# Recurrence: v asked for ahead of the decays, k and r; w1's loads one pair later; combining's first steps behind the diagonals in the last pair

## The chip, the cores and the metric

The kernel runs on one core of one Trainium2 chip. The metric is the device time of one execution in microseconds (us). Three executions of the kernel before took 430.78, 430.81 and 433.74 us (median 430.81).

## What is computed

Three layers, one after the other: a linear recurrence over 768 steps for 4 batches and 8 heads of 48 channels, a soft mixture of 8 experts with 4 slots each, and a dense block with a gated activation.

```python
for t in range(S):                       # S = 768, head_dim 48, float32
    cur = einsum('bhd,bhe->bhde', u * kt, vt)
    y[:, :, t] = einsum('bhd,bhde->bhe', rt, state + cur)
    state = wt * state + einsum('bhd,bhe->bhde', kt, vt)
logits = x @ phi                         # x: 3072 tokens x 384
d = softmax over tokens(logits)          # dispatch: 32 slots
slot_out[e] = relu(slot_input[e] @ w1[e]) @ w2[e]
c = softmax over slots(logits)           # combine
h = (c @ slot_out) @ w_in
out = (h * sigmoid(1.702 * h)) @ w_out
```

## The kernel before

**Stages.** `phase_a` is the recurrence with the logits of the mixture beside it, `phase_b` the experts, `phase_c` the dense block. The change lies in `phase_a` alone. The order of instructions on every engine is the order in which the code is written; nothing reorders it.

**A pair.** The recurrence is cut into 16 pairs: one batch, two heads, all 768 tokens in six chunks of 128. The loop over `i` (L650) interleaves pair `i` with the steps that prepare pair `i+1` and finish pair `i-1`. For one `i` the steps are, with the engine that does each:

- `products(i+1)` (L498 to L501, DVE): two scans over the decays z.
- `diagonal(i, 0)` and `diagonal(i, 3)` (L534, ACT): six activations each that write diagonal matrices `am`; `causal` (L568, DVE) lays the masked `scores` (L562, PE) over them.
- `states(i)` (L549, PE, then a scan L552 on DVE): 10 matmuls that read `v` of pair i. They stand on PE's queue in front of `outputs(i-1, 3)`.
- `outputs(i-1, 0)` and `outputs(i-1, 3)` (L579 reads `am` and `v` of pair i-1, L584 the states and `r`), with a copy L587 on ACT.
- `scale(i+1)` (L507, DVE), `coef(i+1)` (L520, PE), `coef_tr(i+1)` (L527, DVE), and on POOL `unscaled` (L492), the product of r and k in two halves. The small copies `beside` (L487) hold a POOL product back until a named DVE instruction has ended.
- `x_tr(i-1)` (L600, PE; L601, ACT) and `logits` (L810, PE).

**Loads.** All of them are issued by SP, in the order of the code, and an issue that waits holds up those behind it. `load_z` (L466, decays of pair i+3, two buffers), `load_rk` (L473, k and r of pair i+3, four buffers), `load_v` (L480, v of pair i+1, two buffers). So `load_v(i+1)` overwrites v of pair i-1 and has to wait for `outputs(i-1, 3)`; `load_rk(i+3)` overwrites k and r of pair i-1 and waits for the L584 of the same step. Pair 15's k and r are loaded late, at i = 13, for lack of a buffer. The weights w1 (L79, 512 KB each, three in two pairs), w_in (L114, pairs 8 to 13), and at the end w2 (L92) and w1's last expert (L85) fill the gaps.

**The last pair.** At i = 15 `combining` (L886) of the first two batches starts: maximum, difference (DVE L890, L891) and exponential (ACT L892) for each; its second part comes behind `causal(15, 3)`.

The functions that the change touches:

Of the kernel before, what the change touches and what calls it, by code (L numbers as in the profile page):

```python
# [44 lines left out]
NW1 = 7  # L45
# [231 lines left out]
def keep_warm(nc, room, idle, n):  # L277

    for _ in range(n):
        nc.tensor.matmul(room, idle[:, 512:640], idle[:, 0:512], start=True, stop=True)  # L280
# [138 lines left out]
def phase_a(tc, rkz, z0, vin, u_sb, prod, ebias, W, after, late, consts, soft):  # L419
# [5 lines left out]
    with ExitStack() as ctx:  # L425
# [31 lines left out]
        def load_z(p):  # L457
            if p >= n_p:
                return
            st.setdefault(p, {})["z"] = zs[p % 2]  # L460
            if p == 0:
                for c in halves_of_z[::-1]:
                    nc.sync.dma_start(out=zs[0][:, c], in_=z0[:, c])
                return
            for j in range(2):
                nc.sync.dma_start(out=zs[p % 2][64 * j:64 * j + D, :], in_=rkz[p, j, :, 2 * S:])  # L466
# [9 lines left out]
        def load_v(p):  # L476
            if p >= n_p:
                return
            v = vp.tile([128, VW], F32, name="v", bufs=2)
            nc.sync.dma_start(out=v, in_=vin[p])  # L480
            st[p]["v"] = v
# [47 lines left out]
        def diagonal(p, c0):  # L529
            q = st[p]  # L530
            am = q["am", c0] = ap.tile([128, 2, 3, CH], F32, name="am", bufs=3)
            for c in range(3):
                for j in range(2):
                    nc.scalar.activation(am[:, j, c], ident, AF.Copy, scale=q["coef"][:, c0 + c, j:j + 1])  # L534
# [115 lines left out]
        for i in range(n_p + 1):  # L650
            cur, nxt, prv = i < n_p, i + 1 < n_p, 1 <= i
            b1, b2 = batch_of(i - 2), batch_of(i - 3)
            if b2:
                next(peak)
                b2.exponentials()
            elif 2 <= i:
                logits(i - 2)
            if cur and i:
                diagonal(i, 0)
            if cur:  # L660
                keys_tr(i)
            if nxt:
                products(i + 1)
                load_z(i + 3)
            if cur:
                scores(i, 0)
            if b2 and i < n_p - 2:
                b2.token_major()
            if nxt:
                decays(i + 1)  # L670
            peak = b1.peak() if b1 else iter(())
            if prv:
                outputs(i - 1, 0)
            if b1:
                b1.read()
            if b2:
                logits(i - 2)
            if nxt:
                beside(x[:, XL - 1:XL])
                unscaled(i + 1, 1)  # L680
            if cur:
                causal(i, 0)
                states(i)
            next(peak, None)
            if i == n_p - 1:
                rooms = iter([room[:, n * 3 * CH:(n + 1) * 3 * CH] for n in range(3)])
                comb = [bat[1].combining(lambda: sp.tile([128, 3 * CH], F32, name="c4", bufs=3)),
                        bat[0].combining(lambda: next(rooms))]
                for it in comb:
                    next(it)  # L690
            if i == 0:
                keep_warm(nc, psT.tile(), idle, WARM1)
            if cur and i:
                diagonal(i, 3)
            if prv:
                outputs(i - 1, 3)
            if cur:
                scores(i, 3)
            if nxt:
                scale(i + 1)  # L700
            if i < n_p - 4:
                load_rk(i + 3)
            elif i == n_p - 3:
                load_rk(n_p - 1)
            if nxt:
                coef(i + 1)
            if i + 2 < n_p:
                beside(st[i + 1]["rk"][:, S - 1:S])
                unscaled(i + 2, 0)
            if nxt:  # L710
                coef_tr(i + 1)
            load_v(i + 1)
            if n_p // 2 <= i < n_p // 2 + KT * HF // CV:
                W.load_in(i - n_p // 2)
            slots = b2.slots() if b2 and i < n_p - 2 else iter(())
            for _ in range(NC):
                next(slots, None)
            next(peak, None)
            next(peak, None)
            if cur:  # L720
                causal(i, 3)
            if b2 and i == n_p - 2:
                b2.token_major()
            if i == n_p - 1:
                for it in comb:
                    run(it)
            run(slots)
            if prv and i < n_p:
                x_tr(i - 1)
            if i == n_p - 2:  # L730
                W.load2(0)
                W.load2(1)
            if i == n_p - 1:
                W.load1_half(NW1, 1, s2[:, 2 * S:4 * S])
                W.load1_half(NW1, 0, tokens.room(1))
            for m in range(3 * i // 2, min(3 * (i + 1) // 2, KT * NW1)):
                W.load1(*divmod(m, KT))


# [569 lines left out]
```

## Time and profile before

| | us |
|---|---|
| median of three executions | 430.81 |
| the profiled execution | 430.79 |
| its span | 429.0 |
| PE busy | 399.3 |
| DVE busy | 323.5 |
| ACT busy | 261.3 |
| POOL busy | 48.4 |

The span is one execution on the chip; about 1.8 us of the execution's time lie outside it. An engine's busy time is the sum over all stages. The recurrence takes the first 160 us or so, the experts the next 25, the dense block the rest. The profile also has a chain of waits, which goes back from the last instruction, at each step to what released it, and a list of who waited for whom.

### The profile page before, as it was taken

Reading aid. Unit: us, or ns where it says so; the run is one execution under the profiler, and the core shown is the slowest. Engines: PE = TensorE matmul, PEld = TensorE weight load, DVE = VectorE, ACT = ScalarE, POOL = GpSimd, SP = SyncE. Lnnn points to the kernel's source line nnn. Section 1 sums busy time; section 2 is a strip of 40 time slices with the busy share of each in tenths; the row PEclk is TensorE's granted clock in tenths of the full one; section 3 lists DMA queues with packets and bytes.
Section 4 is the critical chain, followed back from the end, with each engine's and each line's share of the span. In section 5 each row is a group of like instructions: output and inputs, shape, how many; then the busy total and the mean of one; then the engine's idle time right before and its main releaser. Section 6 shows DMA issues by size and latency. Waiting matters only on the chain.

```text
span 429.0 us, 8870 instructions
## 1 busy us (share of the span) xinstructions
PE 399.3 (93%) x3402; PEld 305.5 (71%) x3405; DVE 323.5 (75%) x534; ACT 261.3 (61%) x620; POOL 48.4 (11%) x81
## 2 busy tenths in 40 slices
PE   5799989999889989998999999999999999999993
PEld 1566767777667764766887787787888888888872
DVE  7899999999899768959966988777765655743521
ACT  5578677887778656438765666566574544544530
POOL 4423232232222120200000000000000000000000
PEclk9699999999999999999999999999999999999997
DMA  8979879799996979999000001000001543501102
GB/s 218 212 192 252 224 202 236 224 282 277 237 306 205 355 266 402 412 410 422 38 0 0 2 1 37 2 0 20 0 0 53 162 136 93 165 14 61 73 4 82
DMA packets 24565, 67.35 MB, mean 157 GB/s; under 512 B 2848, under 2 KB 6560, under 8 KB 24256
## 3 DMA queue, kind: packets, MB, share of 16 engines
q1 hardware_dynamic: 24512, 66.67, 49.8%
q8 instruction: 29, 0.48, 0.4%
q14 instruction: 24, 0.20, 0.1%
HBM read 61.94 MB, written 4.72 MB: 155 GB/s over the span
## 4 chain that ended last, share of the span: by engine, by line
PE 70%; DMA 11%; DVE 8%; ACT 4%; issue 2%; SPq 1%; POOL 1%; DVEq 0%; ACTq 0%; POOLq 0%
PE po L1127 43%; DMA v<-in_vin 9%; PE pa L1089 5%; PE py L584 3%; PE py L579 3%; PE ps L1006 3%; PE ps L978 2%; DMA wt<-in_rkz 2%; PE pkv L549 2%; PE pg L562 2%; ACT am L534 2%; SPq L473 1%; PE ps L600 1%; DVE gl L1111 1%; PE ps L280 1%
## 5 line engine op out<-in xcount | busy, mean ns | idle before, releaser
L1111 DVE TENSOR_TENSOR gl<-g,gh 128x512 fp32r<-128x512 f32 x96 | 65.4, 688 | 40.5 <-ACT gh L1103 40.2
L1103 ACT CAST gh<-g 128x512 fp32r<-128x512 f32 x96 | 59.4, 619 | 58.9 <-PE po L1127 58.5
L1127 PE MATMUL po<-gh,wi 128*128 128x512 f32 x288 | 88.9, 390 | 0.0
L1127 PE MATMUL po<-gh,wt 128*128 128x512 f32 x288 | 84.0, 391 | 0.0
L534 ACT ACTIVATE am<-con,cT 128x128 f32<-128x128 f32 x192 | 59.4, 392 | 8.2 <-DVE cT L527 8.2
L1127 PEld LDWEIGHTS po<-gh,wi 128*128 128x128 f32 x288 | 54.2, 188 | 11.6
L1127 PEld LDWEIGHTS po<-gh,wt 128*128 128x128 f32 x288 | 54.0, 188 | 11.6 <-issue 0.4
L1096 ACT ACTIVATE g<-pa 128x512 f32<-128x512 f32 x96 | 57.1, 595 | 2.5 <-PE pa L1089 2.5
L1127 PE MATMUL po<-gl,wi 128*128 128x512 f32 x144 | 56.4, 391 | 0.0
L1127 PE MATMUL po<-gl,wt 128*128 128x512 f32 x144 | 51.6, 395 | 1.8 <-DVE gl L1111 1.7
L1089 PE MATMUL pa<-cT,wt 128*128 128x512 f32 x96 | 38.4, 402 | 1.1 <-ACT g L1096 1.1
L568 DVE COPY_PREDICATED am<-con,pg 128x768 f32<-128x768 uint32 x32 | 32.1, 1002 | 3.7 <-ACT am L534 3.7
L1127 PEld LDWEIGHTS po<-gl,wt 128*128 128x128 f32 x144 | 27.0, 188 | 9.2 <-DVE gl L1111 3.5
L1127 PEld LDWEIGHTS po<-gl,wi 128*128 128x128 f32 x144 | 27.0, 188 | 5.7
L492 POOL TENSOR_TENSOR rkb<-wt 128x384 f32<-128x384 f32 x25 | 27.9, 1118 | 13.6 <-DMA wt<-in_rkz 11.3
L501 DVE TENSOR_TENSOR_SCAN wt<-wt 128x774 f32<-128x774 f32 x16 | 28.4, 1772 | 0.5
L498 DVE TENSOR_TENSOR_SCAN wt<-wt 128x774 f32<-128x774 f32 (+1 forms) x17 | 28.1, 1655 | 0.2 <-DMA wt<-in_z 0.2
L579 PE MATMUL py<-am,v 128*64 128x128 f32 x384 | 27.8, 278 | 0.0
L562 PE MATMUL pg<-wt 64*128 64x128 f32 x312 | 25.1, 295 | 0.5 <-DVE am L568 0.5
L601 ACT COPY xb<-ps 128x288 f32<-128x288 f32 x28 | 11.2, 399 | 22.8 <-PE ps L600 22.8
L562 PEld LDWEIGHTS pg<-wt 64*128 64x128 f32 x312 | 20.0, 192 | 5.4 <-issue 2.8
L1147 DVE TENSOR_TENSOR os<-po,wt 128x512 f32<-128x512 f32 x18 | 12.4, 692 | 13.7 <-PE po L1127 13.7
(206 smaller groups left out, 579.1 us busy)
## 6 DMA issues: line engine op xcount, KB each, us to landing
wt<-in_w SPq DMA_DIRECT2D x21, 512.0 KB, 7.3
wt<-in_w SPq DMA_DIRECT2D x13, 768.0 KB, 8.7
wt<-in_rkz SPq DMA_DIRECT2D x26, 288.0 KB, 5.2
v<-in_vin SPq DMA_DIRECT2D x16, 296.0 KB, 5.5
c<-in_wc SPq DMA_DIRECT2D x24, 192.0 KB, 2.5
out_dram<-os SPq DMA_DIRECT2D x18, 256.0 KB, 2.1
wt<-in_rkz SPq DMA_DIRECT2D x30, 145.3 KB, 3.7
wi<-in_w_in SPq DMA_DIRECT2D x6, 512.0 KB, 6.6
```

What stands on the lines that cost most here:

```text
L492: eng.tensor_tensor(out=rkb[:, c], in0=st[p]["r"][:, c], in1=st[p]["k"][:, c], op=ALU.mult)
L498: nc.vector.tensor_tensor_scan(out=sf[:, o:n][:, ::-1], data0=z[:, o + 1:n + 1][:, ::-1], data1=dS[:, o:n][:, ::-1], initial=0.0, op0=ALU. ...
L501: nc.vector.tensor_tensor_scan(out=x, data0=z[:, 0:XL], data1=dX, initial=0.0, op0=ALU.mult, op1=ALU.add)
L534: nc.scalar.activation(am[:, j, c], ident, AF.Copy, scale=q["coef"][:, c0 + c, j:j + 1])
L562: nc.tensor.matmul(q["pg"][:, j, (c - c0) * CH:(c - c0 + 1) * CH], q["k"][64 * j:64 * j + 64, c * CH:(c + 1) * CH], q["r"][64 * j:64 * j + ...
L568: nc.vector.copy_predicated(q["am", c0], later, q["pg"][:, :, 0:3 * CH].rearrange("p j (c t) -> p j c t", t=CH))
L579: nc.tensor.matmul(py[64 * j:64 * j + 64, (c - c0) * CH:(c - c0 + 1) * CH], q["v"][:, c * 96 + j * 48:c * 96 + j * 48 + 64], q["am", c0][: ...
L1089: nc.tensor.matmul(pa, mst[:, f * 128:(f + 1) * 128], cT.at(tb * 512, 512), start=True, stop=True)
L1096: nc.scalar.activation(g, live[n], AF.Gelu_apprx_sigmoid)
L1103: nc.scalar.copy(gh, live[n])
L1111: nc.vector.tensor_tensor(out=gl, in0=g, in1=gh.bitcast(F32), op=ALU.subtract)
L1127: nc.tensor.matmul(live["po", tb][i], w[:, i * 128:(i + 1) * 128], g, start=(f % FH == 0 and k == 0), stop=(f % FH == FH - 1 and k == 2))
```

## The change

Three edits in the loop over `i`. `load_v(i+1)` moves from behind `coef_tr(i+1)` to behind `outputs(i-1, 3)`, and `load_z(i+3)` from behind `products(i+1)` to behind `load_v`; so SP's order in a pair is v, z, k and r, weights instead of z, k and r, v, weights. Each pair loads the parts of w1 that the pair before it used to load. At i = 15 the first part of `combining` is written behind `diagonal(15, 3)`, `outputs(14, 3)` and `scores(15, 3)` instead of ahead of them.

```diff
@@ -661,7 +661,6 @@
                 keys_tr(i)
             if nxt:
                 products(i + 1)
-                load_z(i + 3)
             if cur:
                 scores(i, 0)
             if b2 and i < n_p - 2:
@@ -682,20 +681,22 @@
                 causal(i, 0)
                 states(i)
             next(peak, None)
+            if i == 0:
+                keep_warm(nc, psT.tile(), idle, WARM1)
+            if cur and i:
+                diagonal(i, 3)
+            if prv:
+                outputs(i - 1, 3)
+            load_v(i + 1)
+            load_z(i + 3)
+            if cur:
+                scores(i, 3)
             if i == n_p - 1:
                 rooms = iter([room[:, n * 3 * CH:(n + 1) * 3 * CH] for n in range(3)])
                 comb = [bat[1].combining(lambda: sp.tile([128, 3 * CH], F32, name="c4", bufs=3)),
                         bat[0].combining(lambda: next(rooms))]
                 for it in comb:
                     next(it)
-            if i == 0:
-                keep_warm(nc, psT.tile(), idle, WARM1)
-            if cur and i:
-                diagonal(i, 3)
-            if prv:
-                outputs(i - 1, 3)
-            if cur:
-                scores(i, 3)
             if nxt:
                 scale(i + 1)
             if i < n_p - 4:
@@ -709,7 +710,6 @@
                 unscaled(i + 2, 0)
             if nxt:
                 coef_tr(i + 1)
-            load_v(i + 1)
             if n_p // 2 <= i < n_p // 2 + KT * HF // CV:
                 W.load_in(i - n_p // 2)
             slots = b2.slots() if b2 and i < n_p - 2 else iter(())
@@ -733,7 +733,7 @@
             if i == n_p - 1:
                 W.load1_half(NW1, 1, s2[:, 2 * S:4 * S])
                 W.load1_half(NW1, 0, tokens.room(1))
-            for m in range(3 * i // 2, min(3 * (i + 1) // 2, KT * NW1)):
+            for m in range(3 * (i - 1) // 2 if i else 0, min(3 * i // 2, KT * NW1)):
                 W.load1(*divmod(m, KT))
```

SP's queue in the pairs i = 1 and i = 2, before (775 columns are the decays, 1536 k and r, L79 w1):

```order
L466 DMA wt_79<-in_rkz 48x775 x2
L473 DMA wt_81<-in_rkz 48x1536 x2
L480 DMA v<-in_vin 128x592
L79 DMA wt_82<-in_w 128x1024 x2
L466 DMA wt_79<-in_rkz 48x775 x2
L473 DMA wt_80<-in_rkz 48x1536 x2
L480 DMA v<-in_vin 128x592
L79 DMA wt_83<-in_w 128x1024
```

The same two pairs now:

```order
L480 DMA v<-in_vin 128x592
L466 DMA wt_79<-in_rkz 48x775 x2
L473 DMA wt_81<-in_rkz 48x1536 x2
L79 DMA wt_82<-in_w 128x1024
L480 DMA v<-in_vin 128x592
L466 DMA wt_79<-in_rkz 48x775 x2
L473 DMA wt_80<-in_rkz 48x1536 x2
L79 DMA wt_82<-in_w 128x1024 x2
```

The v of the next pair stands first in each pair, and pair 1 has the one part of w1 that pair 0 had. At the end of the loop the order on SP was, from i = 13 on:

```order
L473 DMA wt_81<-in_rkz 48x1536 x2
L480 DMA v<-in_vin 128x592
L114 DMA wi<-in_w_in 128x512
L79 DMA wt_88<-in_w 128x1024 x2
L480 DMA v<-in_vin 128x592
L92 DMA wt_79<-in_w 128x2x768 x2
L92 DMA wt_80<-in_w 128x2x768 x2
L85 DMA wt_81<-in_w 128x3x512
```

It is now:

```order
L480 DMA v<-in_vin 128x592
L473 DMA wt_81<-in_rkz 48x1536 x2
L114 DMA wi<-in_w_in 128x512
L79 DMA wt_88<-in_w 128x1024
L480 DMA v<-in_vin 128x592
L92 DMA wt_79<-in_w 128x2x768 x2
L92 DMA wt_80<-in_w 128x2x768 x2
L79 DMA wt_88<-in_w 128x1024 x2
L85 DMA wt_81<-in_w 128x3x512
```

Pair 14's v goes ahead of pair 15's k and r, and the last two parts of w1 (1 MB) come behind four loads of w2. On ACT the last pair was, from its key copies on (L543 keys, L587 outputs, L892 combining's exponential, L534 diagonals):

```order
L543 COPY cT_115<-ps_2046 128x384
L587 COPY xt<-py 128x384
L892 ACTIVATE l_1414<-l_1414 128x192
L892 ACTIVATE l_891<-l_891 128x192
L534 ACTIVATE am<-con,cT_115 128x128 x6
L587 COPY xt<-py 128x384
```

It is now:

```order
L543 COPY cT_115<-ps_2046 128x384
L587 COPY xt<-py 128x384
L534 ACTIVATE am<-con,cT_115 128x128 x6
L587 COPY xt<-py 128x384
L892 ACTIVATE l_1410<-l_1410 128x192
L892 ACTIVATE l_887<-l_887 128x192
```

The two exponentials go behind the six diagonals and the second output copy. The order on DVE, PE and POOL is as it was.

## Rows read from the trace of the kernel before

**Rows 1.** The page's 40 slices of 10.7 us: DMA's busy share, and its rate.

```profile
DMA  8979879799996979999000001000001543501102
GB/s 218 212 192 252 224 202 236 224 282 277 237 306 205 355 266 402 412 410 422 38 0 0 2 1 37 2 0 20 0 0 53 162 136 93 165 14 61 73 4 82
```

**Rows 2.** Windows: length, busy PE, PEld, DVE, ACT, POOL; clock, DMA share, GB/s.

```profile
98.00:107.00 9.00, 8.70 (x169) 6.82 (x169) 8.90 (x13) 8.14 (x27) 2.03 (x5) 1.00 1.04 298
...
116.00:125.00 9.00, 7.88 (x120) 5.96 (x116) 8.22 (x8) 6.63 (x20) 2.24 (x4) 1.00 1.00 292
```

**Rows 3.** Waits of PE and DVE, 26 to 163 us: total, times, longest.

```profile
PE pkv L549 <- DMA v<-in_vin: 4.4, 7, 1.0
...
DVE st L552 <- PE pkv L549: 3.0, 6, 0.9
DVE cT L527 <- PE ps L520: 2.3, 6, 0.5
```

**Rows 4.** Chain of waits in pair 3: start, length, what.

```profile
42.09 0.67 PE py L579 x12
...
43.65 0.31 SPq L473
...
44.47 5.32 DMA v<-in_vin
```

**Rows 5.** Timeline, PE, states of pairs 3, 9, 11, 12: start, length; in brackets idle before.

```profile
41.43 0.66 PE L549 MATMUL pkv<-v,cT 128*48 128x48 f32 x20 [0.89 <-DMA v<-in_vin]
...
93.90 0.65 PE L549 MATMUL pkv<-v,cT 128*48 128x48 f32 x20 [0.41 <-DMA v<-in_vin]
...
112.74 0.66 PE L549 MATMUL pkv<-v,cT 128*48 128x48 f32 x20 [0.51 <-DMA v<-in_vin]
...
121.89 0.66 PE L549 MATMUL pkv<-v,cT 128*48 128x48 f32 x20 [1.00 <-DMA v<-in_vin]
```

**Rows 6.** Timeline, DVE: the second scan in two pairs that follow each other.

```profile
31.05 1.77 DVE L501 TENSOR_TENSOR_SCAN wt<-wt 128x774 f32<-128x774 f32 x1
...
39.16 1.77 DVE L501 TENSOR_TENSOR_SCAN wt<-wt 128x774 f32<-128x774 f32 x1
```

**Rows 7.** The page's DMA issues: count, KB of one, median us to landing.

```profile
v<-in_vin SPq DMA_DIRECT2D x16, 296.0 KB, 5.5
```

**Rows 8.** L473 alone, the loads of k and r, 20 to 160 us.

```profile
DMA to landing us min/median/max: 3.5/4.9/6.8
```

**Rows 9.** Timeline of ACT, PE and DVE in the last pair.

```profile
147.46 0.48 ACT L587 COPY xt<-py 128x384 f32<-128x384 f32 x1 [0.67 <-PE py L584]
...
149.43 0.94 PE L562 MATMUL pg<-wt 64*128 64x128 f32 x12
...
149.73 0.36 DVE L891 TENSOR_TENSOR l<-l,mx 128x192 f32<-128x192 f32 x1
...
150.39 1.84 ACT L534 ACTIVATE am<-con,cT 128x128 f32<-128x128 f32 x6
...
152.27 1.02 DVE L568 COPY_PREDICATED am<-con,pg 128x768 f32<-128x768 uint32 x1 [2.18 <-ACT am L534]
...
152.65 0.55 PE L600 MATMUL ps<-con,xt 128*128 128x128 f32 x3 [1.81 <-ACT xt L587]
```

**Rows 10.** Timeline of POOL and DVE: a pair's first product, then pair 15's.

```profile
53.53 1.01 POOL L492 TENSOR_TENSOR rkb<-wt 128x384 f32<-128x384 f32 x1
...
137.46 1.77 DVE L501 TENSOR_TENSOR_SCAN wt<-wt 128x774 f32<-128x774 f32 x1
137.71 2.32 POOL L492 TENSOR_TENSOR rkb<-wt 128x384 f32<-128x384 f32 x1 [3.58 <-DMA wt<-in_rkz]
...
141.14 1.76 DVE L507 TENSOR_TENSOR wt<-wt,wt 128x1536 f32<-128x1536 f32 x1 [0.37 <-POOL rkb L492]
```

**Rows 11.** Timeline, DVE, at the start of the dense block.

```profile
185.60 0.36 DVE L290 TENSOR_SCALAR cv_e<-wt 128x384 int32<-128x384 int32 x1 [2.06 <-DMA wt<-in_w_out]
...
187.63 0.26 DVE L1060 COPY c<-ps 128x96 f32<-128x96 f32 x1 [0.80 <-PE ps L1058]
```

## The prediction

> **What bounds the kernel now.** I read the slices of the page first, then the chain of waits inside the recurrence, then the waits of PE and DVE there, then the timeline of single pairs. The slices [rows 1] show two stages: DMA busy until about 200 us, nearly idle after. The change moves only loads and two ACT instructions of the first 160 us, so the dense block matters only through the moment at which it starts.
>
> In the recurrence the chain runs, pair after pair, through one loop [rows 4]: `outputs` of the pair before (L579) ends, SP issues k and r, SP issues v, v travels 5.32 us, PE starts `states` (L549), and behind that stand the next `outputs`. PE waits for v seven times, 4.4 us in all and 1.0 us at most [rows 3]. Behind a late `states` DVE waits too: 3.0 us at its scan L552, of which the longest (0.9) is the last pair's and has no late v, and 2.3 us at L527 [rows 3]. These waits are PE's, passed on, and are not counted again.
>
> A pair without a late v shows what comes next. The second scan starts at 31.05 and at 39.16 us [rows 6]: 8.11 us, with DVE busy throughout (8.90 of 9.00 us in one of the windows [rows 2]). So a pair cannot go much under 8.1 us, and more than the v waits is not to be had from the loads.
>
> **Part 1, v first.** Before, v of pair 5 was issued at 44.47 us, behind k and r, which start at 43.65, when L584 has ended. It now waits only for L579, which ends at 42.09 + 0.67 = 42.76. That is 44.47 - 42.8 = 1.6 us earlier. The longest wait for v is 1.0 us [rows 3]. So each of the seven waits goes even if v takes as long to land as before; and k and r, 576 KB that went ahead of it, are out of its way. What is late next is PE itself: pair 3's `states` at 41.43 stood idle for 0.89 [rows 5], and without that DVE's 8.11 us governs.
>
> Upper end: all 4.4 us. Lower end: in the pairs that also load w_in (from 88 to 134 us) the DMA engines are full, share 1.04 and 1.00 [rows 2]; there an earlier issue may only mean a longer queue, and the three waits of 0.41, 0.51 and 1.00 us [rows 5], 1.9 together, could stay: 4.4 - 1.9 = 2.5. I take 4.0, near the upper end, since 1.6 us of head start is more than each of the three, and leave 0.4, a fifth of the 1.9, for a queue that has grown.
>
> **Part 2, z later.** z is now issued some 2 us later, behind v. `products` reads it in the pair after the next, over a whole pair (8 us) after its issue: nothing waits for it. Cost 0.
>
> **Part 3, k and r behind v.** k and r land up to 6.8 us after issue [rows 8]; issued at 43.65 and 44.05, that is by 50.9, and POOL first reads them at 53.53 [rows 10]: 2.7 us to spare, a few tenths less once the pairs close up. v's 296 KB [rows 7] now go ahead: at the 298 GB/s of the full window [rows 2] 1.0 us, at the 192 GB/s of the slowest slice of the recurrence [rows 1] 1.5 us. That cover remains; cost 0, and without it each 1 us late would move POOL's product by 1 us.
>
> The exception is pair 15, whose k and r come late as it is: POOL waited 3.58 us for them, ran from 137.71 to 140.03, and DVE's L507 lost 0.37 us [rows 10]. With v of pair 14 ahead they land 1.0 to 1.5 us later. But the product that takes 1.01 us elsewhere took 2.32 beside DVE's scan, ending 0.8 us after the scan's end at 139.23 [rows 10]. Started at 138.7 to 139.2 it ends near 140.2: 0.2 us lost. If it does not catch up, the full 1.5 us is lost. I take 0.3; ends 0 and 1.5.
>
> **Part 4, the exponentials behind the diagonals.** Before, the six diagonals of the last pair started at 150.39, behind the exponentials, which waited for DVE's L891; `causal` stood 2.18 us idle for them, and PE's L600 1.81 us for the copy behind them [rows 9]. Now ACT is free for the diagonals at 147.46 + 0.48 = 147.94; they take 1.84, to 149.8; the copy ends near 150.3. DVE is through with L891 at 150.09 and the scores end at 149.43 + 0.94 = 150.37, so `causal` starts near 150.4 instead of 152.27: 1.9 us. PE's second L600 follows the first at about 150.85 instead of 152.65: 1.8 us. The exponentials run from 150.3 to 151.1, before `causal` ends at 151.4; nobody waits for them. The chain goes on through PE, so I take 1.8. Below, 1.5, if the two exponentials come between a copy L601 and PE; above, 1.9.
>
> **Part 5, w1 later.** w1 still comes at three parts in two pairs, so within the recurrence the DMA engines have no more to do. The last two parts, 1 MB, now stand behind four w2 loads and ahead of w1's last expert and the other w2 loads; at the 402 to 412 GB/s of the slices around 170 us [rows 1] they take 2.5 us of queue. They were in the queue ahead of the w2 loads before, so what is late is only what the queue lost by standing idle then. The first to feel a late stream is w_out: DVE already waits 2.06 us for it, and then has 0.80 us to spare before L1060 needs it [rows 11]. If the engines get there 1.8 us earlier by part 4 and the stream does not follow, 1.8 - 0.8 = 1.0 us is lost. Ends 0 and 1.0; I take 0.2, since the stream starts behind the same `outputs` that part 4 moves forward.
>
> **Sum.** 4.0 - 0.3 + 1.8 - 0.2 = 5.3 us. The profiled execution took 430.79, its span 429.0; the median is 430.81, so the sum carries over: 430.8 - 5.3 = **425.5 us**. With all upper ends, 4.4 + 1.9 = 6.3: 424.5. With all lower ends, 2.5 + 1.5 - 1.5 - 1.0 = 1.5: 429.3.
>
> **Rivals.** *The DMA engines are the bound in the w_in pairs.* For: shares of 1.04 and 1.00 [rows 2]. Against: slices of 0.6 to 0.9 elsewhere in the recurrence [rows 1], and at any pair one or two parts of w1 fewer have been asked for than before. The 1.9 us stay and pair 15's k and r are late by the full 1.5: 430.8 - 2.5 - 1.8 + 1.5 = 428.0. Chance 0.20.
>
> *v lands no earlier.* If v's landing is tied to the weights of the pair before, which now are the last thing ahead of it, the head start is lost and only part 4 remains: 430.8 - 1.8 = 429.0. Against: in pair 3 v's landing followed its own issue by 5.32 us [rows 4], near the median of 5.5 [rows 7], not the weights'. Chance 0.08. The Trainium skill (DMA: Bandwidth & Descriptors, section on queues, rings and completion order) says that a DMA's completion mark lands only after every earlier write of the same DMA engine; by that rule all that was issued before v still counts, and the trace's 5.5 us for 296 KB agrees that it waits for what is ahead.
>
> *Slower: POOL gets between DVE's scans.* If k and r land over 2.7 us later than now, POOL's first product, held at 53.53, slides past `causal` into the next pair's scans. A product takes 1.01 us, and where POOL and a scan met POOL was slowed to 2.32 [rows 10]; if instead the scan loses, each of 11 pairs (4 to 14) gets 1.0 us longer on the engine that has none to spare: 430.8 - 5.3 + 11 = 436.5. It decides from 2.7 us of delay on; v alone is 1.0 to 1.5, so a queue grown by over 1.2 us is needed. Chance 0.06. The Trainium skill (SBUF — State Buffer, section on its two separate sides) says that whichever of the two starts first holds the shared port for its whole instruction; the scan that started at 137.46, ahead of POOL, kept its 1.77 us, which agrees, and no row shows the other order.
>
> **How the numbers follow.** The forecast has 0.62, spread from 424.2 to 426.9; 0.04 is left for a gain beyond that, from pairs that close up further. A measurement here tells about 1% from no change, 4.3 us, so faster means under 426.5. Faster: nine tenths of 0.62 and the 0.04, 0.60. Slower, over 435.1: 0.05. Within 1%: the other 0.35, the first two rivals above all. The range from 424.0 to 428.4 takes in the forecast and the first rival, some 0.8; beyond it lie v landing no earlier (0.08), the slower case (0.06) and a little on either side.
>
> **What would show it.** In the changed profile PE's wait for v is gone or under 0.5 us in total, v's issue stands about 1.4 us after `states` starts, and scans follow each other at 8.1 us in pairs 2 to 5. `causal` of the last pair waits under 0.4 us for ACT. L507's wait for POOL at i = 14 says what pair 15's k and r cost; DVE's wait before L290 of the dense block, longer than 2.06 us, says whether the weight stream fell behind. The prediction is wrong if v waits remain in the w_in pairs, or if POOL's wait for k and r appears in every pair.

## The result, and the profile after

The change takes 427.48 us (median of 4 runs, 424.29 to 428.52) against 432.27 for the kernel before (4 runs, 430.78 to 434.06): ratio 0.9887, 95% interval 0.9852 to 0.9923. Run again with the experiments it took 427.98 (5 runs, 425.64 to 429.48), ratio 0.9898 (0.9856 to 0.9940). Here and below, a ratio and its interval leave out executions more than 1.5% above the fastest of their kernel, and so are not the quotient of the two medians. The profiled execution took 427.10 us, span 425.3; before 430.79 and 429.0. So the profiles differ by 3.7 us. The prediction was 425.5, range 424.0 to 428.4.

The slices of the page, to hold against [rows 1], and the two windows of [rows 2]:

```profile
DMA  8947998899999899999100001000001543502102
GB/s 217 216 104 190 254 265 211 225 272 281 275 246 270 326 389 397 411 416 417 39 0 0 2 1 37 2 0 20 0 0 41 167 142 99 165 1 76 74 4 81
```

```profile
98.00:107.00 9.00, 8.33 (x160) 6.40 (x158) 8.90 (x14) 7.73 (x26) 2.29 (x4) 1.00 1.04 261
116.00:125.00 9.00, 7.51 (x115) 5.72 (x108) 7.69 (x9) 6.35 (x20) 2.01 (x4) 1.00 1.02 245
```

Read the DMA row first: from the fifth slice to the nineteenth the engines are 8 or 9 tenths busy without a gap, where before there were slices of 6 and 7. In the second window their share is 1.02, which is full, at 245 GB/s, and the one wait for v that is left lies in it. The waits of 26 to 163 us, to hold against [rows 3] (total, times, longest), and the one wait for v that is left, in PE's timeline at pair 12:

```profile
POOL rkb L492 <- DMA wt<-in_rkz: 5.5, 1, 5.5
...
DVE st L552 <- PE pkv L549: 2.1, 4, 0.9
...
PE pkv L549 <- DMA v<-in_vin: 1.4, 1, 1.4
...
DVE cT L527 <- PE ps L520: 1.3, 3, 0.5
```

```profile
120.72 0.39 PE L549 MATMUL pkv<-v,cT 128*48 128x48 f32 x8 [1.37 <-DMA v<-in_vin]
```

Seven waits for v, 4.4 us, have become one of 1.4, longer than the longest before. (Before there was an eighth, of 0.30 at pair 10: the profile puts it down to ACT, but v had landed there 0.14 us before PE went on, as in the other seven.) The second scan of pairs 2 and 3 [rows 6], then v on the page [rows 7] and the landings of k and r [rows 8]:

```profile
32.62 1.77 DVE L501 TENSOR_TENSOR_SCAN wt<-wt 128x774 f32<-128x774 f32 x1
...
40.72 1.77 DVE L501 TENSOR_TENSOR_SCAN wt<-wt 128x774 f32<-128x774 f32 x1
```

```profile
v<-in_vin SPq DMA_DIRECT2D x16, 296.0 KB, 5.3
```

```profile
DMA to landing us min/median/max: 4.1/6.2/9.4
```

The scans follow each other at 8.10 us, DVE's own pace, through pairs 2 to 5. The queue is longer: k and r land after up to 9.4 us (6.8 before), v after 4.6 to 8.0 us from 85 to 135 us (5.0 to 6.0 before). The last pair [rows 9] and pair 15's product [rows 10]:

```profile
147.32 1.86 ACT L534 ACTIVATE am<-con,cT 128x128 f32<-128x128 f32 x6
...
148.92 0.94 PE L562 MATMUL pg<-wt 64*128 64x128 f32 x12
149.09 0.46 ACT L587 COPY xt<-py 128x384 f32<-128x384 f32 x1
...
149.45 0.62 ACT L892 ACTIVATE l<-l 128x192 f32<-128x192 f32 x2
149.79 0.87 PE L600 MATMUL ps<-con,xt 128*128 128x128 f32 x6
149.97 1.02 DVE L568 COPY_PREDICATED am<-con,pg 128x768 f32<-128x768 uint32 x1 [0.39 <-PE pg L562]
```

```profile
136.29 1.77 DVE L501 TENSOR_TENSOR_SCAN wt<-wt 128x774 f32<-128x774 f32 x1
...
138.51 1.01 POOL L492 TENSOR_TENSOR rkb<-wt 128x384 f32<-128x384 f32 x1 [5.55 <-DMA wt<-in_rkz]
...
140.63 1.76 DVE L507 TENSOR_TENSOR wt<-wt,wt 128x1536 f32<-128x1536 f32 x1 [1.02 <-POOL rkb L492]
```

The diagonals run ahead of the exponentials, `causal` no longer waits for ACT, and the six L600 run in one piece. POOL's first product of pair 15 begins later than before, and DVE's L507 stands idle for 1.02 us instead of 0.37. The start of the dense block [rows 11]:

```profile
183.69 0.36 DVE L290 TENSOR_SCALAR cv_e<-wt 128x384 int32<-128x384 int32 x1 [2.68 <-PE ps L1006]
...
185.09 0.26 DVE L1060 COPY c<-ps 128x96 f32<-128x96 f32 x1 [0.18 <-PE ps L1058]
```

The first w_out lands at 183.61, 0.08 us before L290, as before (185.52 and 185.60): it is that load that lets it go, though the profile names PE. L1060 has 0.18 us to spare where it had 0.80.

**Where the 3.7 us come from.** The span is cut at the starts of instructions that every kernel here has: `states` of pairs 1, 11 and 15 (T1, T11, T15), the first transposes of combining (L914), the first L1089 and the last L1127. The column "rest" goes to the end of the span; the last column is the execution's time, some 1.8 us more than the span. All in us:

| kernel (profiled execution) | start to T1 | T1-T11 | T11-T15 | T15-L914 | L914-L1089 | L1089-L1127 | rest | us |
|---|---|---|---|---|---|---|---|---|
| before | 23.38 | 89.36 | 34.60 | 9.31 | 35.12 | 229.46 | 7.79 | 430.79 |
| the change | 24.94 | 86.25 | 35.64 | 7.28 | 35.12 | 229.49 | 6.61 | 427.10 |
| the change again | 24.55 | 87.25 | 37.67 | 7.28 | 35.15 | 229.46 | 6.35 | 429.48 |
| v alone | 24.87 | 86.27 | 35.30 | 9.31 | 35.12 | 229.42 | 6.43 | 428.57 |
| combining alone | 24.58 | 89.63 | 34.12 | 7.28 | 37.88 | 229.44 | 7.90 | 432.67 |
| w1 not later | 24.31 | 86.27 | 35.06 | 7.27 | 36.10 | 229.36 | 6.35 | 426.49 |
| w_in spread | 24.84 | 87.21 | 33.55 | 7.27 | 35.18 | 229.50 | 6.39 | 425.71 |
| k, r of 15 first | 25.23 | 86.29 | 34.77 | 7.27 | 36.04 | 229.50 | 6.81 | 427.77 |
| before, even weights | 25.45 | 89.46 | 33.70 | 10.79 | 35.12 | 229.46 | 7.81 | 433.65 |
| v two pairs ahead | 25.30 | 86.34 | 34.09 | 7.28 | 35.56 | 229.49 | 6.38 | 426.21 |
| v ahead, even weights | 24.07 | 86.31 | 33.58 | 7.28 | 35.73 | 229.47 | 6.39 | 424.60 |
| w_in after | 23.65 | 86.28 | 33.54 | 7.28 | 42.92 | 229.52 | 6.40 | 431.44 |
| halves on two queues | 26.04 | 86.32 | 35.17 | 7.27 | 35.39 | 229.50 | 6.63 | 428.09 |

Change against before: +1.56 at the start, -3.11 to pair 11, +1.04 to pair 15, -2.03 in the last pair, 0 to the last matmul, -1.18 behind it: -3.7. Between T1 and the dense block, where it acts, it gains 4.1 us in this execution.

The 1.18 us behind the last matmul come with the program and not with the execution, and no term of the prediction has them. The rest is 7.79 to 7.90 us in the three kernels whose `load_v` stands in the old place (before, combining alone, before with even weights) and 6.35 to 6.81 in all others. In those three SP stands idle for 1.2 to 1.4 us between two of the waits that close the program, in the others for 0.5 at most. Why the place of one load in the recurrence does that stays open.

### The profile page after: what moved, and what is told of

Same layout as the page of the kernel before. It is cut to its first block, busy times and chain, and to the rows that moved or that the text cites. A ratio compares the mean times of both kernels' runs of the same rounds, so it can differ in the third digit from the quotient of the medians.

```text
span 425.3 us, 8885 instructions
## 1 busy us (share of the span) xinstructions
PE 400.4 (94%) x3402; PEld 306.2 (72%) x3405; DVE 322.8 (76%) x534; ACT 260.5 (61%) x620; POOL 47.0 (11%) x81
## 4 chain that ended last, share of the span: by engine, by line
PE 70%; DVE 14%; DMA 7%; issue 3%; ACT 2%; POOL 1%; DVEq 0%; POOLq 0%; SPq 0%
PE po L1127 43%; DMA wt<-in_rkz 5%; PE pa L1089 5%; PE pg L562 3%; PE py L579 3%; PE ps L1006 3%; PE ps L978 2%; PE py L584 2%; DVE am L568 2%; DVE wt L507 2%; DVE wt L498 2%; DMA v<-in_vin 2%; PE ps L600 2%; DVE gl L1111 1%; PE pkv L549 1%
## 5 line engine op out<-in xcount | busy, mean ns | idle before, releaser
L1127 PE MATMUL po<-gh,wi 128*128 128x512 f32 x288 | 88.9, 390 | 0.0
L1127 PE MATMUL po<-gh,wt 128*128 128x512 f32 x288 | 83.9, 391 | 0.0
L534 ACT ACTIVATE am<-con,cT 128x128 f32<-128x128 f32 x192 | 59.5, 392 | 9.8 <-DVE cT L527 9.8
L1127 PEld LDWEIGHTS po<-gh,wi 128*128 128x128 f32 x288 | 54.2, 188 | 11.7
L1127 PEld LDWEIGHTS po<-gh,wt 128*128 128x128 f32 x288 | 54.0, 188 | 11.6 <-issue 0.4
L1127 PE MATMUL po<-gl,wi 128*128 128x512 f32 x144 | 56.4, 391 | 0.0
L1127 PE MATMUL po<-gl,wt 128*128 128x512 f32 x144 | 51.7, 395 | 1.8 <-DVE gl L1111 1.8
L1089 PE MATMUL pa<-cT,wt 128*128 128x512 f32 x96 | 38.5, 402 | 1.1 <-ACT g L1096 1.1
L1127 PEld LDWEIGHTS po<-gl,wt 128*128 128x128 f32 x144 | 27.0, 188 | 9.3 <-DVE gl L1111 3.7
L1127 PEld LDWEIGHTS po<-gl,wi 128*128 128x128 f32 x144 | 27.0, 188 | 5.6
L492 POOL TENSOR_TENSOR rkb<-wt 128x384 f32<-128x384 f32 x25 | 26.7, 1068 | 16.7 <-DMA wt<-in_rkz 13.5
L579 PE MATMUL py<-am,v 128*64 128x128 f32 x384 | 27.5, 278 | 0.0
```

The lines of the kernel that those rows point to most:

```text
L492: eng.tensor_tensor(out=rkb[:, c], in0=st[p]["r"][:, c], in1=st[p]["k"][:, c], op=ALU.mult)
L579: nc.tensor.matmul(py[64 * j:64 * j + 64, (c - c0) * CH:(c - c0 + 1) * CH], q["v"][:, c * 96 + j * 48:c * 96 + j * 48 + 64], q["am", c0][: ...
L1089: nc.tensor.matmul(pa, mst[:, f * 128:(f + 1) * 128], cT.at(tb * 512, 512), start=True, stop=True)
L1127: nc.tensor.matmul(live["po", tb][i], w[:, i * 128:(i + 1) * 128], g, start=(f % FH == 0 and k == 0), stop=(f % FH == FH - 1 and k == 2))
```

## The experiments

**The change again.**

> The changed kernel itself, once more, as the measure for the other kernels of this call. If the late `states` of pair 1 is a run's own (TensorE at half its granted clock until 18 to 21 us), T1 lies anywhere from 23.4 to 24.9 us here, not again at 24.94; from there to L914 it takes 129.2 us within 0.5, with v waits of 1 to 2 us in pairs 12 or 13 alone. If the change made the start late, T1 is 24.9 again.

PE's wait for v, then windows as in [rows 2], first of this execution and then of the first one, then PE's timeline at pair 12:

```profile
PE pkv L549 <- DMA v<-in_vin: 4.4, 2, 2.8
```

```profile
93.00:111.00 18.00, 15.78 (x261) 11.99 (x257) 17.11 (x23) 13.63 (x45) 4.52 (x8) 1.00 1.03 262
111.00:125.00 14.00, 11.07 (x162) 8.39 (x158) 10.66 (x12) 9.61 (x30) 3.46 (x6) 0.90 1.03 254
```

```profile
93.00:111.00 18.00, 16.80 (x284) 12.77 (x279) 17.83 (x25) 14.49 (x47) 4.69 (x9) 1.00 1.04 279
111.00:125.00 14.00, 12.39 (x191) 9.21 (x188) 12.04 (x13) 9.78 (x31) 4.24 (x8) 1.00 1.03 279
```

```profile
122.78 1.04 PE L549 MATMUL pkv<-v,cT 128*48 128x48 f32 x20 [2.81 <-DMA v<-in_vin]
```

A miss: the program is the same, and the waits for v in pairs 10 and 12 are 1.63 and 2.81 us. From T1 to L914 it takes 132.19 us, not 129.2 within 0.5, and gains 1.1 on the kernel before instead of 4.1. The engines' share is the same as in the first execution, their rate lower (262 and 254 GB/s against 279). With the queue full, a lower rate goes with a later v. T1 is 24.55, not again 24.94.

**The parts alone.** *v alone*: only `load_v(i + 1)` moves.

```
             if prv:
                 outputs(i - 1, 3)
+            load_v(i + 1)
             if cur:
                 scores(i, 3)
...
                 coef_tr(i + 1)
-            load_v(i + 1)
```

> Only v is asked for earlier; z, w1 and the combining stay where they were. Measured by the stretch from `states` of pair 1 to the first transposes L914 of the dense block: 133.27 us before, 129.17 us with the whole change. Theory (v's place alone ends the waits for v, z's place costs and brings nothing): the pairs gain what they gained in the whole change, 3.11 us to pair 11 and -1.04 from there to pair 15: 131.2 us, and PE waits for v at pair 12 alone, 1.4 us or so. Rival (z's 291 KB ahead of v hold v up): waits for v of some tenths come back in three or four w_in pairs, 132.0 to 132.6 us. Start: by the theory that the late `states` of pair 1 (24.94 us instead of 23.38) belongs to a run and its granted clock and not to the change, T1 is at 23.4 or 24.9 whichever kernel runs; if it belongs to v's early request, it is near 24.9 here.

429.07 us (10 runs), ratio 0.9928 (0.9896 to 0.9960). T1 to L914: 130.88, and T1 to T11 takes 86.27 against the whole change's 86.25, so z's place ahead of v costs nothing there. PE stood idle for 0.98 us at pair 12 and 0.91 at pair 13, where v had landed 0.13 us before it went on. This kernel also has the short rest, 6.43 us.

*Combining alone*: the block `if i == n_p - 1: rooms = ...` moves behind `scores(i, 3)`, no load moves.

> Only the last pair's first steps of combining are moved behind the diagonals. Theory: the last pair gains what it gained in the whole change, 2.03 us, all of it behind `states` of pair 15: stretch 131.2 us from `states` of pair 1 to L914 (before 133.27), seven waits for v as before, DVE's wait for ACT at `causal` under 0.5 us (before 2.18). Rival (part of the 2.03 comes from the moved loads, since DMA traffic of w1 and of k, r in the last two pairs also differs there): gain of 1.5 us or less, 131.8 us and more. T1 near 23.4 if the late start belongs to the moved loads; 23.4 or 24.9 if it belongs to the run.

429.57 us (10 runs), ratio 0.9937 (0.9908 to 0.9965). T15 to L914 is 7.28, as with the whole change: the 2.03 us are the ACT order's alone. But in the profiled execution (432.67, the longest of the ten) the dense block then waits for the weight stream:

```profile
188.23 0.36 DVE L290 TENSOR_SCALAR cv_e<-wt 128x384 int32<-128x384 int32 x1 [5.73 <-DMA wt<-in_w_out]
```

5.73 - (2.06 + 0.80) = 2.87 us beyond what [rows 11] had to spare, and L914 to L1089 is 2.76 longer. In this execution all that combining gained was lost again; the median of the ten runs is 2.6 us below that of the kernel before.

*w1 not later*: `range(3 * i // 2, min(3 * (i + 1) // 2, KT * NW1))`, as before the change.

> The whole change without its third part: w1's loads come in the pairs in which they came before. Theory (w1's place is worth nothing, since in every two pairs three parts come either way): 129.2 us from `states` of pair 1 to L914, as with the whole change, within 0.3; v's wait of 1.4 us at pair 12 stays. Rival (the delay takes one or two parts out of the full queue ahead of v in the w_in pairs): v waits return there, 0.5 to 1.3 us in sum, 129.7 to 130.5 us. Other way round (the delay pushed two parts into pairs 13 and 14, ahead of k and r of pair 15): L507 at i = 14 waits under 0.5 us for POOL instead of 1.02, stretch 128.6 us.

426.58 us (4 runs), ratio 0.9841 (0.9777 to 0.9906). From T1 to L914 128.60, and L507 waits 0.36 us for POOL (the wait for v is 1.71, at pair 13). These are the figures of the third case, but they do not show that w1's place is the cause: in the second execution of the change, with w1 later, L507 waited 0.36 too. DVE waits 3.95 us for w_out before L290, and L914 to L1089 takes 36.10, 0.98 more:

```profile
183.75 0.36 DVE L290 TENSOR_SCALAR cv_e<-wt 128x384 int32<-128x384 int32 x1 [3.95 <-DMA wt<-in_w_out]
```

Pair 11 to 15 is 0.58 us shorter than with the change and L1089 stands 0.98 later behind L914; the intervals do not tell the two kernels apart.

**What fills the queue.** *w_in after*: the six w_in loads leave pairs 8 to 13.

```
-            if n_p // 2 <= i < n_p // 2 + KT * HF // CV:
-                W.load_in(i - n_p // 2)
...
                 W.load2(1)
+                for m in range(KT * HF // CV):
+                    W.load_in(m)
```

> The whole change, with the six loads of w_in (3 MB) taken out of the pairs 8 to 13 and asked for at i = 14, behind the first w2 loads. Theory (in those pairs v, k and r are late because w_in fills the DMA engines): no wait for v in any pair and L507 at i = 14 waits under 0.4 us for POOL, pair 11 to 15 takes 33.6 us and the stretch from `states` of pair 1 to L914 127.1 us; v lands within 4 us in pairs 9 to 14. The 3 MB then stand in the stream of the last pair, 7.5 us at 400 GB/s, so the dense block's L1089 comes some 6 us later behind L914 than the 35.12 us of the change. Rival (the waits are SP's order or the buffers', not the engines'): a wait for v of 0.5 us or more remains in pairs 9 to 13.

```profile
93.00:111.00 18.00, 16.81 (x289) 12.82 (x285) 17.62 (x24) 14.39 (x47) 4.71 (x9) 1.00 0.93 252
111.00:125.00 14.00, 13.75 (x192) 10.00 (x190) 13.42 (x15) 10.96 (x35) 3.48 (x6) 1.00 0.82 217
```

```profile
DMA to landing us min/median/max: 2.8/3.2/6.1
```

Windows, and v's landing from 85 to 135 us. The share falls below 1, no wait for v is left, L507 waits 0.37:

```profile
137.26 1.76 DVE L507 TENSOR_TENSOR wt<-wt,wt 128x1536 f32<-128x1536 f32 x1 [0.37 <-POOL rkb L492]
```

T11 to T15 takes 33.54, T1 to L914 127.09, as expected: the least that this stretch takes in any kernel here, below called the floor. Two figures missed: v took 6.1 us to land in pair 10 and 4.4 in pair 13, where 4 at most was expected, and the 3 MB cost 7.8 us in the stream instead of 6. The kernel takes 431.58 (8 runs), ratio 0.9977 (0.9948 to 1.0006). So w_in's place in these pairs is the cause of the waits for v that the change left. For k and r of pair 15 that is not shown, since L507 waited only 0.36 in the second execution of the change too.

*w_in spread*: `if i in (1, 2, 3, 7, 8, 13)` in place of 8 to 13.

> The whole change, with the six w_in loads of 512 KB asked for at i = 1, 2, 3, 7, 8 and 13 instead of 8 to 13. Theory (the wait for v of 1.37 us at pair 12 and the late k and r of pair 15 come from DMA engines that w_in fills up, share 1.03 and 1.04 from 93 to 121 us): v lands in 6 us or less in pairs 9 to 14, the wait at pair 12 is gone, L507 at i = 14 waits 0.4 us or less for POOL; pair 11 to 15 takes 35.64 - 1.37 - 0.65 = 33.6 us, the stretch from `states` of pair 1 to L914 127.2 us, the time 2 us under the change's. Rival (the queue is only filled at another place: pairs 2 to 5 have 0.74 to 1.02 of the engines taken): v waits of some tenths each in pairs 2 to 5 give 1 us or more back: 128.2 us and more.

426.36 us (10 runs), ratio 0.9899 (0.9859 to 0.9939). T11 to T15 is 33.55, without a wait for v, but there are waits of 0.52, 0.18 and 1.01 at pairs 4, 5 and 10; T1 to L914 is 128.03, where the theory had 127.2 and the rival 128.2 and more. So the rival is nearer: the waits move when the loads move.

*Even weights*: two parts in each pair from 1 to 13, with the change and without it.

```
-            if n_p // 2 <= i < n_p // 2 + KT * HF // CV:
-                W.load_in(i - n_p // 2)
+            if i in range(2, 13, 2):
+                W.load_in(i // 2 - 1)
...
+            w1n = [0, 1, 3, 4, 6, 7, 9, 10, 12, 13, 15, 16, 18, 19, 21]
+            for m in range(w1n[i], w1n[i + 1]) if i < 14 else ():
```

> The whole change, with the 27 weight loads of the recurrence (21 parts of w1, 6 of w_in, 512 KB each) two to every pair from 1 to 13 and one at pair 0, none behind the first w2 loads. Theory (v of pair 12 and k, r of pair 15 are late because pairs 8 to 13 ask for 2.44 MB each, which the DMA engines can't move in 8.1 to 9.9 us, while pairs 2 to 8 leave a tenth to a quarter of them idle): no wait for v over 0.2 us in any pair, L507 at i = 14 waits 0.4 us or less for POOL; from `states` of pair 1 to L914 127.1 us, and since two parts, 1 MB, leave the weight stream of the last pair, the first w_out lands 2.5 us or more earlier than with the change and DVE's L290 does not wait for it longer than 2.9 us; 2.0 us under the change's time. Rival (the DMA engines are full from pair 4 on, whatever the order, as the wait of 0.52 us at pair 4 and of 1.01 at pair 10 of the run with w_in spread may say): waits for v of 0.3 to 1 us in three pairs or more, 128 us and more, under 1.2 us gained.

With the change: 427.28 us (6 runs), ratio 0.9867 (0.9821 to 0.9914). The profiled execution is the longest of the six (430.44), with 241 GB/s from 93 to 111 us and 5.9 us of waits for v, so it settles nothing between theory and rival and is not in the table; the run with v ahead and even weights, below, asks again.

> The kernel before, with v, z and the combining where they were, and the weight loads spread as two to every pair. Theory (v waited because it stood behind k and r in SP's order, a chain of issue and landing, and only in the w_in pairs also because of the full queue): waits for v remain in most pairs, 2.5 to 4 us in sum, 131.5 to 133 us from `states` of pair 1 to L914 (133.27 before). Rival (the waits for v were the full queue's all along, and the order of v, k and r matters little): v waits fall under 1.5 us in sum and the stretch to 130.5 us or less. The combining costs its 2.0 us in either case.

Without the change: 432.65 us (10 runs), ratio 1.0009 (0.9982 to 1.0036). PE's idle time before `states` remains, 3.9 us in 8 pairs: 2.6 in pairs 2 to 6, 1.3 after. So in the early pairs it was SP's order, as the chain of waits said. T1 to L914 is 133.95, over the expected 133, because the last pair is 1.5 us longer than before. There PE had stood idle for the same 1.81 us before its second L600 [rows 9], but this time the granted clock was 0.50 from 154.5 to 157.9 us, and the twelve matmuls of L579 took 1.55 us where they took 0.88.

**k and r of pair 15 first**: at i = 13, `load_rk(n_p - 1)` ahead of `load_v(i + 1)`.

> The whole change, but at i = 13 k and r of pair 15 are asked for ahead of v of pair 14. Theory (v ahead of them costs the 0.65 us by which pair 11 to 15 is longer behind the wait for v): L507 at i = 14 waits 0.4 us or less for POOL, and v of pair 14, which had 2.2 us to spare, is 2 us later and still in time: from `states` of pair 1 to L914 128.5 us. Rival (what holds k and r up are the weights of pair 12 in the full queue, not v): L507 waits 0.8 us or more as before, 129.2 us. A worse case: v of pair 14 comes too late, PE waits for it 0.3 to 1 us, 129.5 us.

```profile
140.09 1.76 DVE L507 TENSOR_TENSOR wt<-wt,wt 128x1536 f32<-128x1536 f32 x1 [0.35 <-POOL rkb L492]
```

L507 is back at 0.35 us, and v of pair 14 lands 0.26 us before PE needs it. T1 to L914 128.34. But L290 waits 3.87 us for w_out and L914 to L1089 is 0.92 longer: 427.52 us (4 runs), ratio 0.9875 (0.9822 to 0.9929). L507's wait fits the theory, but does not prove it: the second execution of the change had v ahead too and its L507 waited 0.4 us, as it did in every other kernel here but one (0.58, v two pairs ahead). What was won up to L914, the weight stream took.

**v two pairs ahead**, with three buffers for v, one less for x, and k, r of pair 15 first:

```
-            v = vp.tile([128, VW], F32, name="v", bufs=2)
+            v = vp.tile([128, VW], F32, name="v", bufs=3)
...
-            load_v(i + 1)
+            if i == n_p - 3:
+                load_rk(n_p - 1)
+            if i == 0:
+                load_v(1)
+            load_v(i + 2)
```

> The whole change, but v has three buffers instead of two and is asked for two pairs ahead (v of pair i + 2 at the place where v of pair i + 1 stands now), and k, r of pair 15 are asked for ahead of v; the room comes from one of x's buffers. Theory (what is left of the waits for v is a queue of 6.5 to 9.5 us in the w_in pairs, as long as the DMA rate of the execution makes it; v then has 16 us, twice that): no wait for v in any execution, T1 to T15, `states` of pair 1 to `states` of pair 15, at the floor of 119.8 us that the pairs without waits add up to, 127.1 us to L914. The weight stream does not come that much earlier, so DVE's L290 waits 3 to 4.5 us for the first w_out and up to 1.5 us of it is lost; time 1 to 2 us under the change's. Rival (the full queue then makes k and r late, every pair): DVE's L507 waits for POOL in three of the pairs from 9 to 14 or more, 0.5 us and more each, and the gain is under 0.7 us.

426.20 us (6 runs), ratio 0.9883 (0.9832 to 0.9935). No wait for v, at a share of 1.02 from 93 to 111 us: the queue is as full as ever, and PE does not wait for it. T1 to L914 127.70, 0.6 over the floor; L507 waits 0.58 once; L290 waits 3.40 and 0.44 us of it is lost:

```profile
183.31 0.36 DVE L290 TENSOR_SCALAR cv_e<-wt 128x384 int32<-128x384 int32 x1 [3.40 <-DMA wt<-in_w_out]
```

*v two pairs ahead, with even weights:* the two edits together.

> The same as the run with v two pairs ahead, and the weight loads two to every pair from 1 to 13, none behind the first w2 loads. Theory (two parts, 1 MB, leave the stream of the last pair, 2.5 us at its rate): as there, no wait for v, 127.1 us from `states` of pair 1 to L914, and the first w_out lands early enough that L290 waits 2.9 us or less for it: 2 to 3 us under the change's time. Rival (the DMA engines are full from pair 2 to 13, so the parts asked for earlier only push the others back, and k and r with them): waits of POOL for k and r that DVE's L507 feels, and the first w_out no more than 0.7 us earlier than without the spread.

426.69 us (6 runs, 423.11 to 429.99), ratio 0.9866 (0.9814 to 0.9919). No wait for v, T1 to L914 127.16, the floor. L290 at 181.71 waits 3.59 us where 2.9 or less was expected, and the stream still costs 0.61. In the profiles this is the best version, 1.4 us under the change from T1 to the last matmul; by the times it is not told apart from it.

**Halves on two queues**: `(nc.sync, nc.scalar)[j].dma_start(...)` for k, r and z.

> The whole change, but of k, r and of z the second half (partitions 64 to 111) is asked for from ACT's queue, the first (partitions 0 to 47) from SP's, so that the two travel beside each other and not one behind the other. In the recurrence the DMA engines are busy all the time at 260 to 280 GB/s, while the same engines move 405 to 412 GB/s in the weight stream, whose loads write 128 partitions. Theory (a load to partitions 0 to 47 can use half of the ways into the memory, and so holds the 16 engines up; the Trainium skill, SBUF, State Buffer, section on the DMA port swizzle, says that partitions 0 to 63 reach 8 of 16 ports): side by side the two halves of k and r, 576 KB, take about 2 us instead of 3.8, z 1 us instead of 2; the DMA share from 93 to 125 us falls to 0.9 or less, v lands within 4 to 5 us there, PE waits for v under 0.3 us in sum, from `states` of pair 1 to L914 127.1 to 127.6 us, and the start, which waits for the first k and r, comes up to 1.5 us earlier: 424 to 425.5 us. Rival (the loads are slow for another reason, their rows of 6 KB at a pitch of 9244 B or the memory they come from): the share stays at 1.0, waits for v of 1 to 4 us remain in pairs 10 to 13, 129 to 132 us. A cost in either case: ACT issues four loads more in a pair; if one takes it 0.3 us or waits there for a buffer, DVE's `causal` waits for the diagonals in every pair.

```profile
93.00:111.00 18.00, 16.79 (x285) 12.63 (x282) 17.83 (x24) 14.35 (x48) 4.58 (x8) 1.00 1.03 272
111.00:125.00 14.00, 12.33 (x194) 9.51 (x192) 12.31 (x12) 10.65 (x33) 3.46 (x6) 1.00 1.02 275
```

A miss: the share stays at 1.03 and 1.02, a wait for v of 1.54 us at pair 12 stays, T1 is the latest of all. 429.54 us (12 runs), ratio 0.9950 (0.9920 to 0.9980). The cost feared on ACT does not show in the profile: in the recurrence `causal` waits no longer than with the change.

Why do the engines move only 250 to 280 GB/s in the recurrence? The trace's packets say which loads are slow. From 26 to 135 us a row of k or r (6,144 B, to 48 partitions) keeps its DMA engine for 431 to 490 ns on average in every kernel here. In the stream behind the recurrence a row of twice the bytes (12,288 B, to 128 partitions) takes 462 to 469 ns. What stands right behind k and r in the queue is slow as well: v's rows (2,368 B) took 195 ns in the kernel before, where v stood there, and take 125 with the change; the rows of w1 and w_in (4,096 B), which stand there now, took 167 and take 222. With the halves asked for on two queues a row of k or r still takes 431 ns. So asking from two queues does not let the halves travel at twice the rate; whether the 48 partitions are the cause was not tested and stays open.

## Why the prediction came out as it did

The mechanism was the one forecast, and its place. Where the change acts the sum, 5.3 us, was 1.2 too large in the first execution (4.1) and 4.2 in the second (1.1), and the starting value was low. By the medians the change gains 4.8 and 4.1 us, and 1.2 to 1.4 of that is the shorter rest, which no term has: that the total comes so near the sum is in part luck.

- **v waits, 4.0: mis-sized, 2.7 measured.** (That is 3.11 to pair 11, less the 0.37 by which the wait at pair 12 grew.) v is issued 1.36 to 1.41 us after `states` starts, in every pair from 1 on, as said, and that "each of the seven waits goes" holds to pair 11. But the 3.7 us for which PE stood idle there, pair 10's 0.30 among them, are worth 3.1. Before pairs 6, 10 and 11 PE stood idle for 0.18, 0.30 and 0.51 us, and these pairs got 0.01 longer, 0.09 and 0.21 shorter: DVE, which is now idle for 0.1 us or less in each of them, had as much to do. Then "1.6 us of head start is more than each of the three" failed in pair 12: the queue grew by more than the head start, v took 8.0 us to land, and PE waits 1.37 where it waited 1.00. 0.4 had been set aside for a queue that has grown. The row that spoke against it was read, the share of 1.04 and 1.00 [rows 2]; it had no slack in it, and loads asked for earlier by pairs that close up find none. In the second execution the term is worse than nothing: 2.1 us won to pair 11, 3.1 lost from there to pair 15, with L507 as before. By the prediction's own sign, a wait for v that remains in the w_in pairs, this part was wrong in both executions. (The v issued at 44.47 in [rows 4] is pair 4's, not pair 5's; the head start worked out from it is not touched.)
- **The first rival, DMA engines bound in the w_in pairs, is the other half of the truth.** Taking w_in out of them ends every wait for v, moving it moves the waits. Its 1.9 us plus 1.5 for k and r gave 428.0; in one execution it cost 1.37 and 0.65, in the other 4.4 for v, then a stretch at a granted clock of 0.50, and nothing for k and r.
- **k and r of pair 15, 0.3: 0.65** in the first execution, inside its ends of 0 and 1.5. Counted from the start of pair 15's second scan, POOL's first product began at 2.22 us, before at 0.25 [rows 10]: 2.0 us later, where v's bytes alone were reckoned at 1.0 to 1.5. That it then takes 1.01 us and not 2.32 came out as forecast; it ended 0.66 us later than before, and L507 felt all of it. In the second execution it felt nothing. In the pairs between POOL did not wait.
- **Combining, 1.8: 2.03**, the same in all ten profiles of the table that have it, and the ACT order's alone. `causal` waits 0.39 us, for PE and not for ACT.
- **The weight stream, 0.2: 0**, but with only 0.18 us to spare (L1060). The margin read from [rows 11], 2.06 + 0.80, is right to about 0.1 us: waits of 3.95, 3.87 and 5.73 us cost 0.98, 0.92 and 2.76, where 1.09, 1.01 and 2.87 follow from it. That the stream starts behind the same `outputs` does not keep it in step: it was late with combining alone and where w1 was not put off, but also with w1 put off where the recurrence was shorter (k, r of 15 first, v two pairs ahead with and without even weights).
- **z, 0**: right; nothing waits for it.
- **v lands no earlier**: wrong, v of pair 3 was issued at 35.29 and landed at 38.18. The rule of the Trainium skill that stood beside it (DMA: Bandwidth & Descriptors, queues, rings and completion order) fits the full pairs: v of pair 12 landed 1.6 us behind a w1 part that had been asked for 3.8 us earlier (120.58 and 119.02).
- **POOL between DVE's scans**: did not happen; the delay of k and r stayed under its point.
- **The starting value.** The profiled execution of before, 430.79, was near the low end of that kernel's 80 runs (429.33 to 435.05, medians 432.1 to 432.8): T1 came at 23.38, and in the other kernels at 23.65 to 26.04, with or without moved loads. With 432.2 and 5.3 the forecast would have been 426.9.

## What to carry to other kernels

A load asked for earlier lands earlier by its whole lead only while the DMA engines have room; where their share is 1, count the bytes of a pair against the rate of the slowest execution, not the wait against the head start, or give the load a second period of lead. A wait is worth only what no other engine would have filled in the same pair. A stage brought forward needs the stream behind it brought forward too: read the margin of the first consumer, since what exceeds it is lost microsecond for microsecond. And cut the whole span into stretches, the end of the program too, and look at a second execution, before a gain is put down to its cause.

## What the runs showed of the hardware

- From a moment between 9 and 11 us TensorE's granted clock is at 0.50 (1.2 GHz); it rises to 1.00 (2.4 GHz) between 18 and 21 us, differently from execution to execution, while PE does the same work (keep-warm matmuls, then the first pairs' scores and coefficients). Windows 18 to 21 us of before, of the change, of combining alone (no load moved) and of w_in after (loads moved):

```profile
18.00:21.00 3.00, 2.70 (x28) 1.52 (x26) 1.63 (x4) 0.84 (x3) 1.19 (x2) 1.00 0.95 166
```

```profile
18.00:21.00 3.00, 3.00 (x23) 1.56 (x20) 0.64 (x1) 0.00 (x0) 0.19 (x1) 0.50 0.79 177
```

```profile
18.00:21.00 3.00, 3.00 (x25) 1.58 (x24) 1.82 (x2) 0.00 (x0) 0.24 (x2) 0.69 1.02 224
```

```profile
18.00:21.00 3.00, 2.97 (x29) 1.59 (x27) 1.76 (x3) 0.56 (x2) 1.07 (x2) 0.98 1.01 223
```

  T1 follows it: 23.38, 24.94, 24.58, 23.65. So the +1.56 us at the start belong to the two executions compared, and not to the change: with v in its old place T1 is 23.38 to 25.45, with v moved 23.65 to 26.04.
- With PE idle for 2.81 us in the change's second profile the clock fell to its lower level (0.64 in the mean of the 4 us from the end of the wait), and `states` took 1.04 us instead of 0.66. Around the 1.37 us of the first profile it stayed at 1.00. Behind the 1.81 us before the last pair's second L600 it stayed at 1.00 in the kernel before and was 0.50 from 154.5 to 157.9 us in the one with even weights.

```profile
122.70:126.70 4.00, 3.92 (x54) 3.46 (x56) 2.41 (x2) 0.48 (x1) 0.18 (x1) 0.64 0.96 253
```

- The same loads at the same share moved 279 GB/s in one execution and 254 to 262 in another; in the weight stream the engines move 389 to 417.
- In the recurrence a row of 6,144 B to 48 partitions (464 ns with the change) takes its DMA engine as long as one of 12,288 B to 128 partitions in the stream (469 ns). The Trainium skill (SBUF — State Buffer, the DMA port swizzle) says that loads to partitions 0 to 63 reach half of the ports. These rows agree with that, but no run here puts k and r on 128 partitions; asking for the two halves from two queues left the share at 1.03.
